# Stage 1 of two transforms in 64x64 products, with the cosine split and the order rewritten

## The chip, the core and the metric

One core of a Trainium2 chip runs the whole program. Its engines work from their own queues, each strictly in the order in which the program issued to it: TensorE (PE) multiplies matrices into PSUM, ScalarE (ACT) applies functions and copies results out of PSUM, VectorE (DVE) does elementwise work, GpSimd (POOL) does elementwise work between SBUF tensors, and SyncE (SP) issues the DMA transfers. The metric is the device time of one execution in microseconds; lower is better. The kernel before takes 498.01 us, the median of three runs (497.34 to 498.78).

## The reference

The model is a layer of two parts over 2048 tokens of 512 channels, in float32:

```python
x = A_u
h  = x + _A_ref(_layernorm(x), ...)     # a long convolution for each channel
h2 = h + _B_ref(_layernorm(h), ...)     # an expert layer

# _A_ref: K[d,l] = 2 Re sum_n C[d,n] exp(dt A)[d,n]^l   (128 modes for each channel)
#         y = irfft(rfft(u, 4096) * rfft(K, 4096))[:2048];  return y + u * D_skip
# _B_ref: for 32 heads: scores of two 16-entry key tables, the best of each,
#         expert index i1 * 16 + i2;  out = sum_h gelu(x . u[e_h]) v[e_h]
```

So a kernel K of 2048 taps has to be made for each of the 512 channels, both it and the normalized input are transformed to 4096 points, multiplied, and transformed back. Then comes the expert layer, with one expert of 256 for each of 32 heads and each token.

## The kernel before, in words

**First part, the convolution.** The 512 channels are worked in four groups of 128 (c = 0 to 3), and each group in four pieces of 32 channels (kt = 0 to 3). The taps of a channel come from two tables of powers that are multiplied with each other: 32 tables in all (i = 0 to 31, 16 channels each, two for one kt). For a table,

- POOL adds the phases `pg` (L557) from short tables of multiples, and multiplies the magnitudes `mg` (L588 and L594). For four tables together it first makes the short tables (`steps`, `bases`, `powers`, `heads`, L538 to L581).
- ACT takes sine (L647) and cosine (L644 and L645: absolute value, then a sine with a shift) of the phases into PSUM.
- DVE multiplies sines and cosines with the magnitudes, six instructions in four pieces (`sin_g`, `sin_f`, `cos_g`, `cos_f`, L651 to L664). The cosine pieces write over `mg`, the sine pieces write `gf`.
- PE multiplies the two factors (`kgen`, L690, the tile `kps`): 64 instructions for a table. ACT copies two tables' results to `k` (L698), DVE adds the skip term (L702).

`pg`, `mg` and `gf` have two buffers each, so table i can be written only when table i-2 has been used.

**The transforms** go in two stages of matrix products. Stage 1 (`stage1`, L463 to L477) multiplies 32 channels with the constant `c1_s`: the 128 partitions hold four channels of 32 positions, the constant is block diagonal in these four channels, and for each of eight groups g there are two products (real and imaginary part) of 128 rows, 64 output partitions and 128 columns. It runs for the input u (16 times, tile `s1u`, from `xs`) and for the taps (16 times, tile `s1k`, from `k`). Each run is two pieces on PE, of four groups each into one PSUM bank, each with a copy on ACT (L474) to `yu` or `yk`. Stage 2 (L488, tiles `s2yu` and `s2yk`) takes eight pieces for each c. The u result is copied to `U`; the k result is multiplied with U by DVE (`prod`, L732 to L735), for c = 3 with a part on ACT (L739) and on POOL (`rest`, L743). Then `ia` (L764) begins the inverse, and its results go to DRAM (`t_d`, L789) for c < 3 and stay in SBUF for c = 3.

Beside this the weights of the expert layer are folded with the keys (`w_piece`, L828 and L836, 32 pieces), from 512 KB loads on SP.

**Second part.** After the last ia the PSUM and SBUF pools are handed over and eight blocks of 256 tokens are worked: the end of the inverse (`ib`, L1036), layernorm, scores (L1150), selection by comparison (L1280), output. A few small constants are loaded for it (`small`, L938 to L940) and converted (`casts` and `plain`, L943 to L948), and the folded weights are read back from DRAM (`w_q`, L921) and split in a high and a low part (L924, L925).

**What sets the order.** Nothing is scheduled at run time. The function adds 1729 pieces to a plan, each with an engine, a planned cost in us and what it depends on; `plan.run(ORDER)` (L1348) then issues them in the written-out order `ORDER` (L34). The planned costs do not enter the run. Each engine's queue is the subsequence of ORDER that belongs to it. The PSUM pool `psA` has seven banks of 512 float32 for all of the first part.

Of the kernel before, what the change touches and what calls it, by code (L numbers as in the profile page):

```python
# [9 lines left out]
F32 = mybir.dt.float32  # L10
# [9 lines left out]
P = 128  # L20
# [7 lines left out]
def view(t, off, dims):  # L28
# [136 lines left out]
def kernel(ctx, tc, xa, xb, xt, lar, aim, cre, cim, ldt, dsk, wq, ka, kb, ue, ve,  # L165
# [294 lines left out]
    def flat(ps, m):  # L460
        return ps.rearrange("p a b -> p (a b)").rearrange("p (g m) -> p g m", m=m)

    def stage1(dst, lhs8, kt, nm, r, tiles, key):  # L463
        for n in range(2):
            job = {}

            def mm(n=n, job=job):
# [981 lines left out]
```

## Time and profile before

| | |
|---|---|
| median of three runs | 498.01 us (497.34 to 498.78) |
| profiled execution | 499.36 us, its span 497.4 us |
| PE busy | 444.8 us, 89% of the span, 7206 matmul instructions |
| DVE busy | 408.7 us, 82% |
| ACT busy | 296.6 us, 60% |
| POOL busy | 324.7 us, 65% |
| HBM | 46.08 MB read, 13.89 MB written |
| TensorE clock granted | 0.973 of full on average |

The span runs from the first to the last instruction of one execution on the chip. A group line gives busy time, the mean length of one instruction in ns, then the engine's idle time just before these instructions and what ended it. A wait line gives the total, the number and the longest. A stage line (a stretch in us) gives the busy time of each engine within it, the granted clock, the share of the DMA engines and GB/s; with a line number it counts that line alone. A line of time gives start, length and what ran. A float32 product counts as two matmul instructions, each with its own weight load.

### The profile page before, as it was taken

How to read it: one execution, taken by the hardware profiler on the slowest of the kernel's cores; microseconds unless marked ns; L12 is line 12 of the kernel's file. 1: busy time of each engine (PE TensorE's matmuls, PEld its weight loads, DVE VectorE, ACT ScalarE, POOL GpSimd, SP SyncE). 2: the span in 40 equal slices, each digit the busy share in tenths (PEclk: the TensorE clock that was granted, in tenths of full speed). 3: DMA queues.
4: the chain of work that ended last, by engine and by line, in shares of the span. 5: the costliest groups of instructions: out<-in, count | busy, mean ns of one | idle time of the engine just before them, and what ended most of it. 6: DMA issues, size and time to landing. Idle time of an engine off the chain costs nothing.

```text
span 497.4 us, 16692 instructions
## 1 busy us (share of the span) xinstructions
PE 444.8 (89%) x7206; PEld 389.8 (78%) x7206; DVE 408.7 (82%) x708; ACT 296.6 (60%) x594; POOL 324.7 (65%) x344
## 2 busy tenths in 40 slices
PE   0455789999999899999997799999999999999985
PEld 0233679999998889999996788887978888787874
DVE  4998998999879897899766764888979686978994
ACT  6865799859998669966985434463052331416231
POOL 3999899999999998988955203572263516536130
PEclk9977799999999999999999799999999999999999
DMA  7888924670153441400027458210170311010012
GB/s 291 336 270 290 370 64 142 210 253 29 43 193 99 133 130 47 171 3 3 1 88 254 153 179 285 84 47 1 67 246 29 125 49 43 1 45 0 1 54 77
DMA packets 27361, 61.04 MB, mean 123 GB/s; under 512 B 7028, under 2 KB 14456, under 8 KB 26136
## 3 DMA queue, kind: packets, MB, share of 16 engines
q1 hardware_dynamic: 27288, 59.98, 35.0%
q8 instruction: 56, 0.92, 0.8%
q14 instruction: 17, 0.14, 0.1%
HBM read 46.08 MB, written 13.89 MB: 121 GB/s over the span
## 4 chain that ended last, share of the span: by engine, by line
PE 66%; DVE 21%; ACT 4%; DMA 3%; POOL 3%; issue 2%; SPq 0%; DVEq 0%; ACTq 0%; POOLq 0%
PE sc L1150 14%; PE ia L764 12%; PE s2yu L488 6%; PE kps L690 5%; DVE oh L1280 5%; PE s1k L471 4%; PE xu L1157 4%; PE s1u L471 4%; PE s2yk L488 3%; PE ib L1036 3%; DMA wq<-wq 2%; PE o L1327 2%; PE cnt L1290 2%; PE wps L828 2%; DVE U L733 2%
## 5 line engine op out<-in xcount | busy, mean ns | idle before, releaser
L557 POOL TENSOR_TENSOR pg<-PS 128x1024 int32<-128x1024 int32 x32 | 68.8, 2151 | 0.1
L588 POOL TENSOR_TENSOR mg<-TS 128x1024 f32<-128x1024 f32 x32 | 62.5, 1959 | 9.3 <-PE kps L690 9.1
L1280 DVE TENSOR_SCALAR oh<-idxb,ec_s 128x2048 bf16<-128x2048 bf16 (+1 forms) x72 | 50.3, 757 | 6.8 <-ACT idxb L1262 6.8
L764 PE MATMUL ia<-ca_s,U 128*128 128x128 f32 x256 | 51.1, 282 | 0.5 <-POOL U L743 0.5
L1192 POOL TENSOR_TENSOR ks<-kq 128x512 f32<-128x512 bf16 x16 | 17.2, 1078 | 46.5 <-DVE kq L1186 45.5
L1060 POOL TENSOR_TENSOR vs<-hc 128x256 f32<-128x256 f32 x8 | 6.6, 829 | 61.8 <-ACT hc L1083 61.8
L645 ACT ACTIVATE t<-t,halfpi 128x512 f32<-128x512 f32 x64 | 42.4, 662 | 2.1
L1150 PE MATMUL sc<-w_hi,hhi 128*128 128x480 f32 x128 | 42.2, 410 | 0.0
L764 PEld LDWEIGHTS ia<-ca_s,U 128*128 128x128 f32 x256 | 40.3, 199 | 0.8 <-POOL U L743 0.8
L644 ACT ACTIVATE t<-pg 128x512 f32<-128x512 int32 x64 | 39.1, 610 | 2.5 <-DVE gf L652 2.2
L647 ACT ACTIVATE t<-pg 128x512 f32<-128x512 int32 x64 | 37.9, 609 | 2.9 <-POOL pg L557 1.3
L1150 PE MATMUL sc<-w_lo,hhi 128*128 128x480 f32 x128 | 38.4, 380 | 0.0
L1150 PE MATMUL sc<-w_hi,hlo 128*128 128x480 f32 x128 | 38.4, 381 | 0.0
L764 PE MATMUL ia<-ca_s,yk 128*128 128x128 f32 x192 | 38.2, 281 | 0.0
L594 POOL TENSOR_TENSOR mg<-TS 128x512 f32<-128x512 f32 x32 | 37.4, 1172 | 0.2
L828 PE MATMUL wps<-wq,ka_s 128*32 128x128 f32 x200 | 12.4, 326 | 25.1 <-DMA wq<-wq 22.0
L690 PE MATMUL kps<-mg 128*32 128x64 f32 x1024 | 33.5, 229 | 1.0 <-DVE mg L660 0.7
L488 PE MATMUL s2yk<-yk,c_s 128*128 128x128 f32 x256 | 32.6, 279 | 1.4 <-DVE U L735 0.7
L690 PE MATMUL kps<-gf 128*32 128x64 f32 x1024 | 32.9, 226 | 0.0
L471 PE MATMUL s1u<-c_s,xs 128*64 128x128 f32 x512 | 31.8, 276 | 1.1 <-DVE xs L508 0.7
L488 PEld LDWEIGHTS s2yk<-yk,c_s 128*128 128x128 f32 x256 | 30.2, 192 | 3.1 <-ACT yk L474 1.3
L488 PE MATMUL s2yu<-yu,c_s 128*128 128x128 f32 x256 | 31.4, 277 | 0.0
(198 smaller groups left out, 1390.9 us busy)
## 6 DMA issues: line engine op xcount, KB each, us to landing
wq<-wq SPq DMA_DIRECT2D x25, 512.0 KB, 4.8
t_d<-T SPq DMA_DIRECT2D x24, 256.0 KB, 3.9
Tb<-t_d SPq DMA_DIRECT2D x8, 768.0 KB, 7.1
x<-xa SPq DMA_DIRECT2D x8, 512.0 KB, 5.8
xs<-xb SPq DMA_DIRECT2D x16, 256.0 KB, 4.0
xt<-xt SPq DMA_DIRECT2D x8, 512.0 KB, 5.7
out<-ob SPq DMA_DIRECT2D x7, 512.0 KB, 3.0
c_s<-wq SPq DMA_DIRECT2D x4, 512.0 KB, 9.5
```

Of the source, the lines that this page charges most:

```text
L471: T.matmul(ps[64 * k:64 * k + 64, g, :], lhs8(4 * n + g), c1_s[:, k], start=True, stop=True)
L488: T.matmul(ps[:, k, :], c2_s[:, kk, :], y[:, :, kk, :], start=True, stop=True)
L557: G.tensor_tensor(view(pg, 0, [[32, 2 * NC], [8, 4], [1, 8]]), view(t["PS"], 1024 + off, [[1, 2 * NC], [128, 4], [0, 8]]), view(t["PS"], 8 ...
L588: G.tensor_tensor(view(mg, 0, [[96, NC], [8, 8], [1, 8]]), view(ts, 512 + 8 * o, [[8, NC], [1, 8], [0, 8]]), view(ts, 8 * o, [[8, NC], [0, ...
L594: G.tensor_tensor(view(mg, 64, [[96, NC], [8, 4], [1, 8]]), view(ts, 1536 + o, [[1, NC], [64, 4], [0, 8]]), view(ts, 1024 + 8 * o, [[8, NC ...
L644: A.activation(p, pg[:, :, k], AF.Abs)
L645: A.activation(p, p, AF.Sin, scale=-SINSCALE, bias=halfpi)
L647: A.activation(p, pg[:, :, k], AF.Sin, scale=SINSCALE)
L690: T.matmul(kps[32 * q:32 * q + 32, 2 * g + h, :], m[:, d, 64:96], m[:, d, 0:64], start=(e == 0), stop=(e == 1))
L764: T.matmul(ps[:, g, :], t[:, 4 * n + g].rearrange("p a b -> p (a b)"), ca_s[:, s, :], start=(s == 0), stop=(s == 1))
L1150: T.matmul(ps[:, 512 * h:512 * h + 480], t[x_][:, q, ts], I[w_][:, q, 480 * h:480 * h + 480], start=(q == 0 and x_ == w_), stop=(q == 3 an ...
L1280: V.tensor_scalar(oh[:, :, 0:ln], t["idxb"][:, :, sl], S["ec"][:, 4 * e + j:4 * e + j + 1], None, op0=ALU.is_equal)
```

## The change

Three things change.

*Stage 1.* The constant loses half its columns: instead of one block-diagonal block of four channels (128 columns) it holds two blocks of two channels, one in the upper 64 partitions and one in the lower 64 (64 columns). A group g now has four products, of 64 rows, 64 output partitions and 64 columns: row half h times real or imaginary part k. The row half h writes to bank h. All eight groups of a run are one piece on PE that takes two banks, with 64 matmul instructions in place of two pieces of 16. Each bank is then copied on its own by ACT; since a bank now holds two of the four channels d of every (g, k), the copy writes two elements out of every four.

*Cosine.* The absolute value and the shifted sine become two pieces of the plan, so that other ACT work can stand between them. The sines and cosines no longer follow each other through a common key.

*Order.* The plan has 1761 pieces and a new ORDER. On PE the ia pieces of c = 0 to 2 stand one to three at a time between the `kgen` pieces (before: in longer runs in places), and at the end of the first part stand kgen 30, kgen 31, stage 1 of pieces 1 and 3 of group 3, then stage 2; before: kgen 30, stage 1 of pieces 2, 1 (half) and 0, kgen 31, the rest of 1, and 3, then stage 2. On POOL `bases` of table 8 stands before `mg` of table 4 (before: after it). On DVE `casts` and `plain` stand ahead of the eight products of c = 3 (before: after the first copies of ia, c = 3). On SP the loads `small` come after the first t_d stores of c = 2 and one cb load, ahead of the w_q loads (before: after these). From ia of c = 3 on, the PE queue is the same but for a few places in the first blocks.

```diff
 ORDER = (
-    0, 17, 1, 2, 3, 4, 5, 6, 71, 72, 8, 16, 18, 19, 20, 21, 23, 24, 7, 87, 22, 29, 25, 35, 59, 36, 37, 30, 26, 38, 27,
...
+    0, 2, 1, 3, 4, 5, 71, 76, 66, 11, 9, 13, 87, 6, 18, 19, 17, 24, 20, 23, 27, 72, 25, 21, 22, 26, 29, 30, 35, 36,
...
-    c1_s = wk.tile([P, 2, 128], F32, name="c1_s")
+    c1_s = wk.tile([P, 2, 64], F32, name="c1_s")
...
     def stage1(dst, lhs8, kt, nm, r, tiles, key):
-        for n in range(2):
-            job = {}
-
-            def mm(n=n, job=job):
-                ps = bank(job, f"{nm}_{n}")
-                for g in range(4):
+
+        job = [dict(), dict()]
+
+        def mm():
+            ps = [flat(bank(job[h], f"{nm}_{h}"), 64) for h in range(2)]
+            for g in range(8):
+                for h in range(2):
+                    rows = slice(64 * h, 64 * h + 64)
                     for k in range(2):
-                        T.matmul(ps[64 * k:64 * k + 64, g, :], lhs8(4 * n + g), c1_s[:, k], start=True, stop=True)
-
-            def ev(n=n, job=job):
-                A.copy(dst()[:, 8 * kt + 4 * n:8 * kt + 4 * n + 4].rearrange("p g k d -> p g (k d)"), job["ps"])
-
-            k = plan.add("PE", 0.99, mm, r=r + ["c1"], t=tiles, take="psA", n_mm=16)
-            plan.add("ACT", 0.48, ev, w=[key + (kt, n)], t=tiles, give="psA", after=[k])
+                        T.matmul(ps[h][64 * k:64 * k + 64, g, :], lhs8(g)[rows], c1_s[rows, k], start=True, stop=True)
+
+        def ev(h):
+            A.copy(dst()[:, 8 * kt:8 * kt + 8].rearrange("p g k (h d) -> p h (g k) d", h=2)[:, h],
+                   job[h]["ps"].rearrange("p a b -> p (a b)").rearrange("p (a d) -> p a d", d=2))
+
+        k = plan.add("PE", 0.96, mm, r=r + ["c1"], t=tiles, take=("psA",) * 2, n_mm=64)
+        for h in range(2):
+            plan.add("ACT", 0.64, lambda h=h: ev(h), w=[key + (kt, h)], t=tiles, give="psA", after=[k])
...
-        def trig(k, cos):
-            p = t_k[k, cos] = flat(bank(t_k, f"t{k}{cos}_{i}", (k, cos, "ps")), 32)
-            pg = t["pg"]
-            if cos:
-                A.activation(p, pg[:, :, k], AF.Abs)
+        def trig(k, cos, part=0):
+            pg = t["pg"][:, :, k]
+            if part < 2:
+                t_k[k, cos] = flat(bank(t_k, f"t{k}{cos}_{i}", (k, cos, "ps")), 32)
+            p = t_k[k, cos]
+            if part == 1:
+                A.activation(p, pg, AF.Abs)
+            elif cos:
                 A.activation(p, p, AF.Sin, scale=-SINSCALE, bias=halfpi)
             else:
-                A.activation(p, pg[:, :, k], AF.Sin, scale=SINSCALE)
+                A.activation(p, pg, AF.Sin, scale=SINSCALE)
...
-            a = plan.add("ACT", cost, lambda k=k, cos=cos: trig(k, cos), r=[("pg", i)], w=["trig"], lag=0.2,
-                         t=tiles, take="psA")
+        for k, cos, fn, dcost in ((0, 0, sin_g, 1.2), (1, 0, sin_f, 0.6), (0, 1, cos_g, 1.2), (1, 1, cos_f, 0.6)):
+            a = plan.add("ACT", 0.61 if cos else 0.52, lambda k=k, cos=cos: trig(k, cos, cos), r=[("pg", i)], lag=0.2,
+                         t=tiles, take="psA", tab=None if cos else "trig")
+            if cos:
+                a = plan.add("ACT", 0.62, lambda k=k: trig(k, 1, 2), t=tiles, tab="trig", after=[a])
...
-    c1 = np.zeros((4, 32, 2, 32, 4))
+    c1 = np.zeros((4, 32, 2, 32, 2))
     for q in range(4):
-        c1[q, :, 0, :, q] = np.cos(a)
-        c1[q, :, 1, :, q] = -np.sin(a)
+        c1[q, :, 0, :, q % 2] = np.cos(a)
+        c1[q, :, 1, :, q % 2] = -np.sin(a)
```

More of the change, by code (lines that the diff above doesn't have):

```diff
@@ L664, in cos_f @@
             V.tensor_mul(mg[:, :, f_], mg[:, :, f_], t_k[1, 1])
-        for k, cos, cost, fn, dcost in ((0, 0, 0.52, sin_g, 1.2), (1, 0, 0.52, sin_f, 0.6),
-                                        (0, 1, 1.22, cos_g, 1.2), (1, 1, 1.22, cos_f, 0.6)):
-            a = plan.add("ACT", cost, lambda k=k, cos=cos: trig(k, cos), r=[("pg", i)], w=["trig"], lag=0.2,
-                         t=tiles, take="psA")
+        for k, cos, fn, dcost in ((0, 0, sin_g, 1.2), (1, 0, sin_f, 0.6), (0, 1, cos_g, 1.2), (1, 1, cos_f, 0.6)):
[3 more added lines that the diff above has]
+                a = plan.add("ACT", 0.62, lambda k=k: trig(k, 1, 2), t=tiles, tab="trig", after=[a])
             w = [("tab", i, k, cos)] + ([("mgf", i, k)] if cos else [])
@@ L1396, in _constants @@
     f = np.float32
-    return s, dict(c1=c1.reshape(128, 256).astype(f), c2=c2.reshape(128, 4096).astype(f),
+    return s, dict(c1=c1.reshape(128, 128).astype(f), c2=c2.reshape(128, 4096).astype(f),
                    ca=ca.reshape(128, 256).astype(f), cb=cb.reshape(128, 64, 64).astype(f),
```

164 rows, old and new, of the table ORDER are left out of this document.

## The prediction, made before the change was run

> **What bounds the kernel now.** I read the slices first, then busy time by stage, then who waits for whom, then the chain.
>
> ```profile
> PE   0455789999999899999997799999999999999985
> POOL 3999899999999998988955203572263516536130
> ```
>
> Forty slices of 12.4 us. GpSimd (POOL) is nearly full from the second slice to the twentieth, while it builds the 32 kernel tables; after that it is mostly idle and the second half belongs to TensorE (PE). Both lines are full in the same stretch, so the busy shares by stage are needed:
>
> ```profile
> core 0: us, PE busy (x) PEld busy (x) DVE busy (x) ACT busy (x) POOL busy (x), PEclk, DMA share, GB/s
> 60.00:255.00 195.00, 188.28 (x3685) 175.43 (x3687) 174.55 (x290) 164.67 (x319) 184.08 (x166) 1.00 0.30 102
> ```
>
> From 60 to 255 us PE works 188.3 of 195, POOL 184.1, VectorE (DVE) 174.6, ScalarE (ACT) 164.7. Two engines stand at the limit; the waits say which one holds the other.
>
> ```profile
> engine line waited for: us in total, times, longest us
> POOL mg L588 <- PE kps L690: 9.1, 6, 2.4
> ```
> ```profile
> 54.29 1.95 POOL L588 TENSOR_TENSOR mg<-TS 128x1024 f32<-128x1024 f32 x1 [2.20 <-PE kps L690]
> ...
> 191.44 1.96 POOL L588 TENSOR_TENSOR mg<-TS 128x1024 f32<-128x1024 f32 x1 [2.37 <-PE kps L690]
> ...
> 253.79 1.20 POOL L594 TENSOR_TENSOR mg<-TS 128x512 f32<-128x512 f32 x1
> 265.90 1.28 POOL L743 TENSOR_TENSOR U<-ki,U 64x512 f32<-64x512 f32 x1 [10.91 <-DVE yu L732]
> ```
>
> POOL's magnitude table `mg` has two buffers, so table i waits for the products `kps` of table i-2. PE reaches these late six times, 9.1 us in all: 2.2 at 54 us, the other 6.9 after 60. All else on POOL is its own work, back to back. So **POOL sets the pace until its last table piece ends at 255.0 (call that T), and PE, being late, takes 9.1 us of it.** The chain past T:
>
> ```profile
> 254.21 4.52 PE s1k L471 x80
> 258.72 1.03 PE kps L690 x64
> 259.75 2.90 PE s1k L471 x48
> ...
> 263.32 1.17 PE s2yk L488 x8
> ...
> 264.51 0.59 ACT ki L739
> ...
> 265.13 0.70 DVE yu L732
> ```
>
> From T to stage 2 (263.32) it is 8.3 us. Then DVE's eight products run back to back, and the rest (ia, and the whole expert part) hangs on their end.
>
> **The change, part by part.** *Stage 1 on PE.* A job (one transform, one channel group) was 32 instructions on 128 columns; it becomes 64 on 64 columns, each with half the rows. Now:
>
> ```profile
> 60.00:255.00 195.00, 53.00 (x880) 47.62 (x882) 1.00 0.30 102
> ```
>
> This is stage 1 (L471) alone: 53.00 us for 880 instructions, 60 ns each; back to back 4.52/80 = 56.5 ns, so 1.81 us a job. No row of before shows 64-row products side by side, so the new job is bounded. From below: L690 above issues 64 instructions on 64 columns, four column strips at once, in 1.03 us, 16.1 ns each. From above: if the two row halves take turns, only pairs overlap, and 32 pairs at the 64.4 ns that L690 takes for a group of four give 2.06 us. I take 1.03 us, because count, columns and four-fold packing are those of L690. In the stretch from 60 to 255 there are 880/32 = 27.5 jobs: 53.0 - 27.5 x 1.03 = 24.7 us less for PE, 163.6 instead of 188.3 us (upper bound: 27.5 x 0.25 = 7 us more). The Trainium skill has a rule against this: "TensorE: Matmul & The Clock Gate", Part 1, says that matmul starts never come closer than about 25 ns. By it the job would take 64 x 25 = 1.6 us, and PE would gain only about 6 us by that estimate. The row of L690, 16.1 ns, contradicts it for strips that work side by side.
>
> *What PE's 24.7 us are worth.* At most what POOL waited for PE, 9.1 us. They are spread over the whole stretch, 0.8 us at each job, against lateness of at most 2.4 us at a time, and the new order puts the inverse's ia pieces in ones, twos and threes between the kps instead of in runs. For the wait at 54 us the new order also sets one more piece of POOL work (`bases` of table 8, here at 71 us: 2.0 us together) ahead of that mg.
>
> ```profile
> 71.02 0.28 POOL L548 COPY PS<-A 128x128 int32<-128x128 int32 x1
> 71.38 1.71 POOL L550 TENSOR_TENSOR PS<-PS 128x128 int32<-128x128 int32 x3
> ```
>
> What remains: kps also waits for DVE's and ACT's table pieces, and DVE has 174.6 us to do in what becomes some 188, 93%.
>
> ```profile
> 80.00:180.00 100.00, 97.70 (x1935) 90.79 (x1935) 90.10 (x147) 81.52 (x162) 97.12 (x92) 1.00 0.38 126
> ```
>
> From 80 to 180 us POOL was 97.1% busy beside a PE at 97.7%, with hardly a wait. From 180 to 255:
>
> ```profile
> POOL mg L588 <- PE kps L690: 6.3, 4, 2.4
> ```
>
> I let the later part become like this one and leave 2.5 us of waits: **-6.6 us**. Ends: -9.1 and 0.
>
> *Evictions on ACT.* Each still moves 512 elements a partition, but writes runs of two elements in every four instead of one run of 512.
>
> ```profile
> 60.00:255.00 195.00, 31.34 (x56) 1.00 0.30 102
> ```
> ```profile
> L772 ACT COPY T<-ia 128x512 f32<-128x512 f32 x24 | 13.8, 592 | 1.2 <-PE ia L764 1.1
> L474 ACT COPY yk<-s1k 128x512 f32<-128x512 f32 x32 | 17.8, 592 | 1.6 <-PE s1k L471 1.4
> ```
>
> L474 in the stretch: 31.34/56 = 0.56 us each. L772 writes runs of four elements and takes the same 592 ns as L474's long run, so short runs alone cost nothing down to four. For two: from below 0.56, from above twice 592 = 1.18 us (a pair costs what four did). I take 0.72: the diff raises its planning price from 0.48 to 0.64, and the 0.16 is added to the row. ACT: 164.7 + 56 x 0.16 = 173.6 us, 92% of 188. It has cover: 0 on the end. The Trainium skill, "SBUF — State Buffer" (its note on SBUF cachelines), gives lines of 16 bytes that run at full rate with two hits each; two of four fp32 are two hits, so by it ACT would stay at 164.7. That changes no term of the sum, only the odds of a full ACT.
>
> *Cosine in two pieces.* The same two activations (L644, L645), now with room for other ACT work between them; no work is added. If the pieces are pulled apart, DVE gets a cosine later by one eviction, 0.6 us. The cover is DVE's other work:
>
> ```profile
> DVE gf L651 <- POOL mg L588: 4.1, 6, 1.5
> ...
> DVE mg L664 <- ACT t L645: 1.6, 4, 0.7
> DVE mg L659 <- ACT t L645: 1.6, 4, 0.5
> ```
>
> These are DVE's waits from 60 to 255 us (total, times, longest): it waited 3.2 us for cosines in 64 of them. 0; without the cover +1, two or three such delays at the last tables.
>
> *The tail past T.* L664 of the last table and kps stay as they are; after kps come k131 and k133 in 2 x 1.03 us instead of 2.90 (-0.8), but five evictions stand on ACT behind the last kps copy at about 0.64 apart instead of some 0.52 (+0.6): **-0.2 us**.
>
> ```profile
> 260.30 2.09 ACT L474 COPY yk<-s1k 128x512 f32<-128x512 f32 x4
> ```
>
>
> *A wait that the new order adds.* DVE's four small casts (`casts`, `plain`, L943 on) stood at 290 us, after ia began; now they stand ahead of the eight products. They need the three little loads of L938 to L940, which on SP's queue stand behind a run of t_d stores and one cb load.
>
> ```profile
> 290.27 0.18 DVE L943 CAST key_s<-key_f 128x30 bf16<-128x30 f32 x1
> ```
> ```profile
> 254.02 3.16 SPq L789 DMA_DIRECT2D t_d<-T  x4
> ...
> 264.03 2.56 SPq L789 DMA_DIRECT2D t_d<-T  x4
> ...
> 279.72 0.64 SPq L938 DMA_DIRECT2D key_f<-keys  x1
> 280.40 0.43 SPq L939 DMA_DIRECT2D ec_s<-ecode  x1
> 280.87 0.43 SPq L940 DMA_DIRECT2D hs_f<-hsel  x1
> ```
> ```profile
> hs_f<-hsel SPq DMA_DIRECT2D x1, 16.0 KB, 3.7
> ```
>
> The last eviction of ia2 stands on ACT just ahead of cosine of table 31, so the stores go out from about T+1.5; 2.6 to 3.2 us of issue, 0.4 for cb, and then 1.5 for the three: the last is issued near T+6.5 and, by 3.7 us, lands at T+10.2. The first product could start at 265.13 - 255.0 - 0.2 = T+9.9; the casts, about 0.5 us, end at T+10.7. Behind the casts wait all eight products, then POOL's L743, ia, everything. **+0.8 us**; ends 0 (the load lands early) and +4 (SP waits for freed memory).
>
> *Elsewhere.* c1 is half as large (one small DMA of many). The start is reordered, but POOL begins its tables near 8.7 us, after the same ka load; DVE's step of the first 64 modes comes first, so its new first piece should be fed in time: 0, ends -1 and +2.
>
> ```profile
> 8.39 0.21 POOL L280 TENSOR_TENSOR ka_s<-ka_s 128x15 f32<-128x15 f32 x1 [6.93 <-DMA ka_s<-ka]
> 8.57 0.21 POOL L280 TENSOR_TENSOR kb_s<-kb_s 128x15 f32<-128x15 f32 x1
> ```
>
> From ia3 on the queues are nearly unchanged: 0.
>
> Sum: -6.6 - 0.2 + 0.8 = -6.0. The profiled execution took 499.36 us (span 497.4 and 1.96 around it), 1.35 above the median of 498.01. 499.36 - 6.0 = 493.4, and at the median **492.0 us**.
>
> **Rivals.** (1) *All waits go*: POOL never waits, the casts are in time: 498.0 - 9.1 - 0.2 = 488.7. For it: PE falls to 87%. Against: DVE and ACT both go above 90%.
> (2) *The gain is hidden*: kps comes late through DVE or ACT instead, or the casts hold up 3 us or more, and POOL gets back 0 to 3 us: about 496. For it: DVE at 93% in a fixed order. Against: POOL's waits for kps are those that the trace names, and DVE itself waited 4.1 us for POOL's mg.
> (3) *ACT becomes the bound*, slower: without stage-1 evictions ACT has 164.7 - 31.3 = 133.3 us in the stretch; with 56 evictions of p us it fills the present 195 us at p = 1.10. From there the kernel is slower than before. At p = 1.18 ACT needs 199.4 us even if never idle: 498 + 4.4 = 502.4. Against: L772's 592 ns. The Trainium skill's "TensorEngine Tiling (Array Packing)", on the PSUM bottleneck, warns that the copy out of PSUM may take over once the products are packed; ACT's 85% in the stretch is the room there is.
> (4) *The row halves do not overlap*: jobs of 2.06 us, PE 188.3 + 7 = 195.3 us, so it is the bound with an order written for less: 498 + 7 = 505. Against: column strips do overlap in L690 (16.1 ns each).
>
> **How the numbers follow.** Forecast (489.5 to 494.5) 0.48; rival 1 0.14; rival 2 0.24; rival 3 0.06; rival 4 0.08. A measurement here tells 0.3% (1.5 us) from no change. Faster means below 496.5: 0.48 + 0.14 + 0.13 of rival 2 = 0.75; same is the remaining 0.11 of rival 2; slower is 0.14, rivals 3 and 4. Range 487.5 to 499.0: all of the forecast and of rival 2, nearly all of rival 1.
>
> **What would show it.** Right: stage 1 at about 1.0 us for 64 instructions; POOL's wait for kps below 4 us; T near 248.5; PE some 25 us less busy before T; ACT's L474 line between 0.6 and 0.8 us each. Wrong: a job near 1.8 or 2.0 us; L474's successor above 1.1 us; T unmoved; a DVE wait of several us for a small load (key_f or hs_f) ahead of the first product; or POOL waits of the old size with another name before them.

## The result, and the profile after

The changed kernel takes **513.51 us** (median of 4 runs, 511.23 to 514.53) beside 498.39 us for the kernel before on the same chip (497.34 to 499.05): ratio 1.0299, 95% interval 1.0259 to 1.0339. The forecast was 492.0, the range 487.5 to 499.0. The profiled execution has a span of 511.4 us, 14.0 more than before.

The slices of the changed kernel's page, 40 of 12.8 us, for TensorE and GpSimd:

```profile
PE   1556778989988979787996599999999999999986
POOL 3999888996999988996971601564053625445130
```

GpSimd has eights and sixes among its nines now and stays at its tables a little longer; TensorE, which stood at nine from the seventh slice to the twenty-first with one eight, now has sevens and eights there. Busy time by stage of the changed kernel (length; then busy us of PE, PEld, DVE, ACT and POOL with their instructions; granted clock, DMA share, GB/s), first the same 195 us as before, then up to the new end of the tables:

```profile
60.00:255.00 195.00, 168.18 (x4290) 153.41 (x4291) 165.67 (x270) 154.14 (x300) 174.86 (x157) 0.96 0.32 108
60.00:265.00 205.00, 178.18 (x4507) 162.98 (x4508) 174.15 (x284) 163.96 (x318) 184.73 (x163) 0.97 0.30 103
```

TensorE is busy 20 us less in the 195 us, and the other engines got less done too: GpSimd 174.9 us of work where it had done 184.1. It needs the next 10 us for the same 184.7. The last table piece, the start of stage 2 and the last ia, from the timeline (the first two rows) and the chain of the changed kernel:

```profile
263.72 1.15 POOL L600 TENSOR_TENSOR mg<-TS 128x512 f32<-128x512 f32 x1
...
275.72 8.83 PE L494 MATMUL s2yk<-yk,c_s 128*128 128x128 f32 x64 [1.20 <-ACT yk L478]
```
```profile
290.62 16.80 PE ia L774 x126
```

T is 264.87 where it was 254.99: **+9.9**. From T to stage 2 it is 10.85 us where it was 8.33: **+2.5**. From there to the last ia 14.90 for 13.99: +0.9. From ia to the end 220.8 for 220.1: +0.7. Together the 14.0 us. What GpSimd waited for from 60 us to T in the changed kernel (total, times, longest):

```profile
POOL mg L594 <- PE kps L700: 9.5, 7, 3.8
POOL pg L563 <- ACT t L656: 4.0, 1, 4.0
POOL mg L594 <- ACT t L656: 1.5, 1, 1.5
POOL mg L594 <- DVE xs L514: 0.9, 1, 0.9
POOL mg L594 <- DVE gf L661: 0.4, 1, 0.4
```

That is 16.3 us; in the same stretch of before it was 6.9 for kps and 0.2 for DVE. The waits for kps (the products of `kgen`; the expectations below call them the key products), which the change was to take away, have grown by 2.6. The larger part of the 9.2 us more is new: 5.5 for ScalarE, and 1.1 more for DVE. So TensorE, busy for less time, is later than before. Its own waits in the first 300 us of the changed kernel show what it is late for; "issue" means that it waited for nothing that the profile shows:

```profile
PE kps L700 <- issue: 5.8, 4, 2.2
...
PE s1u L475 <- issue: 4.4, 4, 2.1
PE s1k L475 <- issue: 2.1, 3, 1.2
```

12.3 us, in the two groups of products that have 64 columns. The kernel before has one such row in that stretch, 0.6 us in other products. These stretches of "issue" are called stops from here on. Eleven of them are over 0.25 us; nine lie on the chain of waits ahead of the last ia, 11.3 us together (before: one, 0.6). How one of these gaps sits on the path shows in the chain of waits of the changed kernel (start, length, what, how many products):

```profile
206.13 1.09 PE s1k L475 x64
207.22 0.57 PE wps L838 x16
207.80 1.81 PE s1k L475 x105
209.61 0.70 issue
210.31 0.57 PE s1k L475 x23
210.89 1.65 PE kps L700 x104
212.54 2.19 issue
214.73 0.59 PE kps L700 x24
```

After 185 products without a pause the engine stops inside a job, waiting for no other engine; it goes on for 127 products (23 + 104), stops again for 2.2 us, and goes on. The same happens behind T: the chain has 1.82 us of "issue" at 268.22 and 1.15 at 272.34 (rows below), 3.0 us together, which is more than the +2.5.

```profile
268.22 1.82 issue
270.04 0.97 PE kps L700 x51
271.01 1.33 PE s1k L475 x77
272.34 1.15 issue
```

51 + 77 = 128 products between the two. The DMA queue that brings instructions, of before and then of after (packets, MB):

```profile
q8 instruction: 56, 0.92, 0.8%
```
```profile
q8 instruction: 64, 1.05, 0.9%
```

The changed kernel's page counts 8230 products and as many weight loads on TensorE: 16,460 instructions in 64 packets, 257 each (before: 2 x 7206 in 56, 257). The 2048 instructions by which the two differ are 8 packets, 256 each. So a packet is about 128 products with their loads, if the queue serves mostly TensorE. That is the distance between the stops. The theory formed from this, called SUPPLY in the runs: *TensorE uses narrow products up faster than the packets come, and a long run of them empties its store.* Its rival, ORDER: *the written-out order is what costs the time, whatever the products are.*

### The profile page after: what moved, and what is told of

Its sections match the earlier page's. It is cut to its first block, busy times and chain, and to the rows that moved or that the text cites. A ratio compares the mean times of both kernels' runs of the same rounds, so it can differ in the third digit from the quotient of the medians.

```text
span 511.4 us, 18756 instructions
## 1 busy us (share of the span) xinstructions
PE 438.0 (86%) x8230; PEld 378.9 (74%) x8230; DVE 409.3 (80%) x708; ACT 296.3 (58%) x594; POOL 325.7 (64%) x344
## 4 chain that ended last, share of the span: by engine, by line
PE 51%; DVE 19%; ACT 10%; POOL 9%; issue 6%; DMA 4%; SPq 0%; DVEq 0%; POOLq 0%; ACTq 0%
PE sc L1160 11%; PE ia L774 9%; DVE oh L1290 4%; PE s2yu L494 4%; PE kps L700 4%; PE s2yk L494 3%; PE xu L1167 3%; PE s1u L475 3%; PE o L1337 2%; PE cnt L1300 2%; DVE U L743 2%; PE ib L1046 2%; ACT t L654 2%; PE s1k L475 2%; DMA wq<-wq 2%
## 5 line engine op out<-in xcount | busy, mean ns | idle before, releaser
L700 PE MATMUL kps<-mg 128*32 128x64 f32 x1024 | 36.2, 233 | 6.5 <-DVE mg L673 3.2
L700 PE MATMUL kps<-gf 128*32 128x64 f32 x1024 | 35.1, 230 | 4.0 <-issue 4.0
L494 PE MATMUL s2yk<-yk,c_s 128*128 128x128 f32 x256 | 35.3, 293 | 3.1 <-ACT yk L478 1.2
L494 PEld LDWEIGHTS s2yk<-yk,c_s 128*128 128x128 f32 x256 | 32.3, 204 | 4.6 <-ACT yk L478 1.3
L700 PEld LDWEIGHTS kps<-mg 128*32 128x32 f32 x1024 | 26.5, 116 | 11.8 <-issue 10.1
L494 PE MATMUL s2yu<-yu,c_s 128*128 128x128 f32 x256 | 33.4, 282 | 0.8 <-DVE U L745 0.8
L494 PEld LDWEIGHTS s2yu<-yu,c_s 128*128 128x128 f32 x256 | 30.8, 195 | 2.2 <-PE wpt L846 1.0
```

The lines of the kernel that those rows point to most:

```text
L494: T.matmul(ps[:, k, :], c2_s[:, kk, :], y[:, :, kk, :], start=True, stop=True)
L700: T.matmul(kps[32 * q:32 * q + 32, 2 * g + h, :], m[:, d, 64:96], m[:, d, 0:64], start=(e == 0), stop=(e == 1))
```

## The experiments

**Two orders, three kinds of product.** The change altered the products and the order at once. Four kernels take them apart. The first keeps the order of before; each run's two pieces become one, at the place of the first:

```
 ORDER = (as before, stage-1 pairs merged at the first one's place)
 stage1: as in the changed kernel (64x64 products, two banks, strided copies); cosine in one piece
```

> Stage 1 in 64x64 products with its strided copies, but the order of before (each stage-1 run stands where its first half stood) and the cosine in one piece. Two theories. SUPPLY: PE runs out of instructions after long runs of narrow products (idle time on PE that nothing in the trace ends), and PE's lateness then reaches ACT, DVE and POOL. It expects such gaps here too, 5 to 12 us in sum, and 496 to 506 us. ORDER: the new order is what costs, the products are fine. It expects no gaps that matter, POOL waiting under 4 us for kps, and 489 to 494 us.

The second has the changed kernel's order with the products of before:

```
-  T.matmul(ps[h][64*k:64*k+64, g, :], lhs8(g)[rows], c1_s[rows, k], ...)   # 32 products of 64 columns
+  T.matmul(ps[n][64*k:64*k+64, g, :], lhs8(4*n + g), c1_s[:, k], ...)      # 16 products of 128 columns
```

> The kernel after (new order, cosine split), but each stage-1 run does the products of before: 16 products of 128 rows and 128 columns (32 instructions) into two banks, and two copies in long runs. SUPPLY expects no gap over 0.5 us without a releaser on PE; PE has some 25 us more to do, so 500 to 509 us, below the 513.5 of after. ORDER expects no gain from it: 513 us or more, since PE is slower and the order the same.

The third and fourth leave stage 1 out as a computation:

```
+  T.matmul(ps[h][64*k:64*k+64, g, :], bf16(lhs8(..)), bf16(c1_s[:, k]), ...)  # 16 products of 256 columns
```

> The kernel after, but stage 1 is left out as a computation: each run fills the same two banks with 16 bf16 products of 256 columns (16 instructions in place of 64, about 0.9 us of PE time in place of 1.03; the values are not the transform's). Copies, order and cosine as after. SUPPLY expects 488 to 497 us and hardly a gap without a releaser. ORDER expects 510 to 515 us, as after.

> As oldorder_64, but stage 1 is left out as a computation: 16 bf16 products of 256 columns in each run, the same banks and strided copies. It shows what 25 us less of PE work are worth in the order of before without the narrow instructions. SUPPLY expects 488 to 493 us and several us less than oldorder_64; ORDER expects the same time as oldorder_64 within 1.5 us.

| | before's products (32 instructions a run) | 64x64 (64 instructions) | bf16 (16 instructions) |
|---|---|---|---|
| order of before, two pieces | 498.4 | not run | 499.0 (below) |
| order of before, merged | 514.9 (below) | 517.01, ratio 1.0348 [1.0308, 1.0389] | 509.87, 1.0204 [1.0153, 1.0256] |
| new order | 519.63, 1.0375 [1.0311, 1.0438] | 513.51, 1.0299 [1.0259, 1.0339] | 499.57, 1.0014 [0.9992, 1.0036] |

None of the four times is in the range that SUPPLY gave for it, and of those that ORDER gave only that of the second run is (513 us or more). So neither theory is right as it stood. In the new order the same place, banks, copies and cosines cost nothing against before when stage 1 has few instructions, and 13.9 us more when it has many. The two have nearly the same work on TensorE from 60 to 255 us: stage 1 alone in the bf16 kernel and in the changed kernel (length; PE and PEld busy with instructions; clock, DMA):

```profile
60.00:255.00 195.00, 33.72 (x464) 25.37 (x464) 0.98 0.31 107
```
```profile
60.00:255.00 195.00, 36.29 (x1728) 31.73 (x1728) 0.96 0.32 108
```

33.7 and 36.3 us busy, 464 and 1728 instructions. 2.6 us of work do not by themselves make 13.9 us of time. What differs much is the number of instructions, and the form of the products, which the next run keeps. The granted clock differs too: from 80 to 120 us it is 0.91 in the changed kernel and 1.00 in the bf16 one; what that is worth was not taken apart. In the bf16 kernel GpSimd waits 2.9 us for kps from 60 us to T, and T is 252.9:

```profile
POOL mg L600 <- PE kps L706: 2.9, 2, 2.2
```

But that kernel does not reach 492 either. Its last ia starts at 274.25 us, 3.1 earlier than before; the rest takes 222.9 us for 220.1, and in it TensorE stops for 2.6 us at ib (before: 0.4). ORDER is wrong for the loss in the new order, and SUPPLY alone does not explain the missing gain. With the products of before the new order is slowest of all, as ORDER had it: GpSimd waits 13.8 us for kps and 8.5 for ScalarE there. That this order was written for runs of 1 us and gets runs of 1.8 is a likely reason that no run shows. That kernel also has a stop of 2.3 us at s1u, where SUPPLY gave none over 0.5; it comes 21 products behind 128 kps products in a row. The new order sets two kps jobs side by side in three places; the order of before does so once. In the merged old order every column is slow, 11.5 us even with bf16; that is taken up below.

**Half the instructions, the same tiles.** Bf16 also changes the form of the products. The next run keeps fp32, the 64x64 tiles, banks, copies and order, and gives each product 128 columns, so that 32 instructions move the same columns. Every second group is computed with its neighbour's weights.

```
-  for g in range(8):  T.matmul(ps[h][.., g, :], lhs8(g)[rows], c1_s[rows, k], ...)                  # 64 columns
+  for g in range(4):  T.matmul(ps[h][.., g, :], lhs8(2*g)[rows], c1_s[rows, k] twice side by side)  # 128
```

> The changed kernel with its 64x64 tiles, its banks, its strided copies and its order, but every stage-1 run made of 16 fp32 products of 128 columns in place of 32 of 64 columns: half the instructions (32 for 64), and by the estimate 32 instructions of 128 columns over four tiles the same columns through the array. What is left out: every second group of eight is computed with the weights of its neighbour. Theory SUPPLY (TensorE runs out of instructions in long runs of narrow products): the idle time of TensorE without a releaser behind stage-1 and key-product lines falls from 12.3 us in the first 300 us to under 5, GpSimd's waits for the key products from 11.4 us to about 4 to 6, and the time from 513.5 to 498 to 505 us. Rival TILES (products in 64x64 tiles themselves hold up the products around them, however many instructions they are): idle time and waits stay, 510 to 515 us. Rival ORDER (the new order alone costs the time): 510 us or more.

506.74 us (505.58 to 508.66), ratio 1.0157 [1.0110, 1.0204]: 6.8 us below the changed kernel with equal work, and 7.2 above the bf16 one; just over the upper end that SUPPLY gave, as are GpSimd's waits for kps (7.5 us, where 4 to 6 were expected). TensorE's gaps in the first 300 us of this kernel:

```profile
PE s1u L475 <- issue: 3.8, 1, 3.8
...
PE kps L701 <- issue: 0.9, 1, 0.9
...
PE s1k L475 <- issue: 0.7, 1, 0.7
```

5.4 for 12.3 us, in three stops, each soon after one of the three runs of 128 kps products in a row (they begin at 101.6, 208.7 and 263.1 us). The rival that 64x64 tiles are themselves in the way falls; 64, 32 and 16 instructions a run give 513.5, 506.7 and 499.6. The last ia starts at 290.62, 283.88 and 274.25 us in these three, and the stops on the chain ahead of it are 11.3, 5.4 and 1.6 us. So of the 16.4 us between the first and the third 9.7 are stops that stand on the chain; the rest is not placed by these runs. A part may be what follows from a stop: GpSimd's long wait for ScalarE, which ends at 123 to 129 us, is 4.0 us in the changed kernel, 5.7 here and 7.4 with the products of before, each time behind stops at 104 to 112 us, and the bf16 kernel has neither; how one leads to the other was not followed.

**The products by themselves.** A program of its own runs narrow products back to back on data that lies ready, with 12 wide products ahead of each section.

> A program of its own, not the kernel: after 12 wide products each, five runs of TensorE alone on data already in place: (a) 384 fp32 products in four column strips of 32, 128 rows, 64 columns, the form of the key products; (b) 384 in 64x64 tiles of 64 columns, the form of the changed stage 1; (c) 192 of 128 rows, two column tiles of 64, 128 columns, the form of the stage 1 before; (d) 192 in 64x64 tiles of 128 columns; (e) the strips of (a) again while 12 loads of 512 KB run. It computes nothing of the reference. Theory SUPPLY expects (a) and (b) to start at about 16 ns per instruction for the first hundreds of instructions and then to break up into stretches with idle gaps of 0.5 to 2.5 us, about 3.4 us for each 256 instructions in the long run (768 instructions: over 12.4 us by one gap or more), no gap in (c), at most a short one in (d), and (e) not better than (a). If (a) and (b) run through in about 12 to 13 us without a gap, SUPPLY in this form is wrong and the gaps have to do with the kernel around them.

The timeline of the second section, 64x64 tiles with 64 columns, then sections three and four (128 columns; 128-row products, then 64x64 tiles):

```profile
58.02 2.79 PE L53 MATMUL b<-a 64*64 64x64 f32 x175
61.71 2.09 PE L53 MATMUL b<-a 64*64 64x64 f32 x128 [0.90 <-issue]
65.44 2.09 PE L53 MATMUL b<-a 64*64 64x64 f32 x128 [1.64 <-issue]
69.17 2.09 PE L53 MATMUL b<-a 64*64 64x64 f32 x128 [1.64 <-issue]
72.62 2.09 PE L53 MATMUL b<-a 64*64 64x64 f32 x128 [1.36 <-issue]
```
```profile
99.28 21.18 PE L58 MATMUL b<-a 128*64 128x128 f32 x384
...
140.82 10.71 PE L63 MATMUL b<-a 64*64 64x128 f32 x384
```

175 products run through, then exactly 128 at a time, with a stop between. Inside a stretch a product takes some 16 ns; from the start of one stretch to the next it is 3.45 to 3.73 us, or 27 to 29 ns a product. Sections three and four have no stop: 21.18/384 = 55 ns, and 10.71/384 = 27.9 ns, which is just what the supply gives. Stops in total, of the sections with 32-wide strips, with 64x64 tiles, and with strips beside 6 MB of loads:

```profile
PE b L73 <- issue: 10.1, 5, 3.1
PE b L45 <- issue: 7.7, 5, 1.7
PE b L53 <- issue: 6.9, 5, 1.6
```

This is SUPPLY without the kernel around it; beside the loads the stops are 2.4 us longer, in this one execution.

The trace also has the packets of the instruction queue, 16,384 bytes each. In the second section:

| packet, from and to (us) | TensorE goes on at | after the packet's end |
|---|---|---|
| 59.36 to 60.40 | 61.71 | 1.31 |
| 62.84 to 64.14 | 65.44 | 1.30 |
| 66.56 to 67.89 | 69.17 | 1.28 |
| 70.30 to 71.25 | 72.62 | 1.37 |

Each stop ends 1.3 to 1.4 us after a packet has come in, and the next packet starts 1.1 us after TensorE goes on. It is so in the kernels as well: the two stops behind T in the changed kernel end 1.44 and 1.41 us after packets that came in at 268.60 and 272.08 us, and in all 18 profiles 97 of the 98 stops of over 0.25 us end 1.2 to 1.6 us after a packet. So what TensorE waits for in a stop is instructions. The Trainium skill, "Runtime: NRT & Kernel Launch", section "Instruction fetch mechanics", says that instructions are refilled in blocks of 16 KiB (256 instructions), and that this is hidden because engines dispatch more slowly than the refill. The trace agrees with the block (stops 128 products apart, 16.4 KB a packet) and not with the hiding: 256 instructions are used up in 2.09 us and refilled in 3.45 to 3.73.

**What the relief of TensorE is worth.** The kernel before, with nothing changed but the bf16 products: two pieces, one bank each, contiguous copies, same order, TensorE's stage 1 busy for 36.0 us in place of 53.0 in the 195.

```
-  T.matmul(ps[64*k:64*k+64, g, :], lhs8(4*n + g), c1_s[:, k], ...)            # 8 fp32 products a piece
+  T.matmul(ps[64*k:64*k+64, g, :], bf16(lhs8(..)), bf16(c1_s[:, k]), ...)     # 8 bf16 products, 256 columns
```

> The kernel before with nothing changed but the products of stage 1: two pieces, one bank each, the contiguous copies and the order all stay; each piece is 8 bf16 products of 256 columns in place of 8 fp32 products of 128 columns, so that stage 1 as a computation is left out and TensorE is relieved by some 0.4 us per piece, 64 pieces. This is the relief that the prediction counted on, without narrow products and without a new order. The prediction's own term (waits of GpSimd for the key products go, -6.6 us) expects 490 to 493 us and waits of GpSimd for key products under 3 us. Theory ORDER in its strong form (a written-out order gives back what one engine gains) expects 496 us or more, the waits still near 9 us. An addition of time is expected by neither.

498.99 us (496.81 to 503.06, 10 runs), ratio 1.0002 [0.9972, 1.0031]: **nothing**. GpSimd's waits in the first 300 us of this kernel:

```profile
POOL mg L595 <- PE kps L697: 3.6, 3, 1.7
POOL mg L595 <- DVE k L709: 3.1, 1, 3.1
```

The waits for kps fell by 5.5 us. But at 55 us a wait of 3.1 us for DVE stands where one of 2.2 us for kps stood, so all these waits together fell from 9.3 to 6.7 us, by 2.6 where the prediction counted 6.6. Stage 2 starts at 260.36, 3.0 earlier. These 3 us are gone at the end. Its chain of waits, in the second part:

```profile
354.57 1.67 PE ib L1043 x119
356.24 2.27 issue
358.52 0.35 PE ib L1043 x9
```

The inverse's last step, ib, has 128 narrow products in a run; here they stop after 119 of them.

**Where the packets end.** In the kernel before there is 0.4 us of such stops at ib. Is that chance? The same kernel profiled again:

> The kernel before, unchanged, profiled once more: whether the idle gaps of TensorE in the inverse transform's narrow products of the second part (0.4 us in the first profile of this kernel, 1.6 to 6.5 us in four of the other runs) come and go between executions of one program. If they do, this profile shows 1 us or more there, or its second part (from the last quarter's inverse transform to the end, 220.1 us in the first profile) differs by over 1 us; if they belong to the edited kernels, it shows 0.4 us and 220 us again.

499.04 us, span 497.1, 0.4 us of stops at ib again. So they look like a property of the program, as far as two profiles can tell. If they depend on where a packet ends, moving all instructions on by part of a packet must move them. One early product group, in an idle stretch, is done three or five times over:

```
-  for a, k_s in ((0, ka_s), (1, kb_s)):
+  for a, k_s in ((0, ka_s), (1, kb_s)) * (3 if n == 0 else 1):      # or 5
```

> As oldorder_halves_few (the kernel before, stage 1 as a computation left out: two pieces, their banks, copies and order as before, bf16 products of 256 columns), and the first product group of the key weights, at 9.7 us, is done three times in place of once, with the same result: 64 more instructions with their weight loads, while TensorE waits for a load there (idle from 10.8 to 16.3 us). All later instructions of TensorE stand 64 further on in their stream, a quarter of a 256-instruction packet. Theory BLOCK (the idle gaps inside the narrow products of the second part, 2.3 us in oldorder_halves_few, depend on where a packet of 256 instructions ends within them) expects the gaps in those narrow products of the inverse transform to change by 1 us or more, and the time with them: 496 to 498 us if they go, 500 to 502 us if they grow. Rival STATE (they depend on how fast TensorE got there, not on the place in the stream) expects 2 us of gaps again and 498 to 500 us.

> As few_shift2 with five times in place of three: 128 more instructions, half a packet. BLOCK expects gaps that differ from those of oldorder_halves_few and of few_shift2 by 1 us or more in at least one of the two, and a time that follows; the prediction's term for the relief of TensorE alone (3.0 us that the first part did gain) would then show as 495.5 to 497 us in the one without gaps. STATE expects 2 us and 498 to 500 us.

> The kernel before with the first product group of the key weights done five times in place of once: the same result, 128 more instructions of TensorE in an idle stretch. BLOCK expects idle gaps of 1.5 us or more in the second part's narrow products, where the kernel before had 0.4 in both of its profiles, and 499.5 to 502 us; if the shift costs the first part nothing and the gaps stay away, 498 to 499 us, as STATE expects.

> The changed kernel with the same shift of 128 instructions. SUPPLY (sustained supply is below what long runs of narrow products ask for) expects the gaps in the first part to move but not to go: 10 to 14 us of idle time without a releaser in the first 300 us, and 511 to 516 us. If the place in the packets were all there is to it, the time falls to 505 us or below, or rises over 519.

With 64 instructions more, the bf16 kernel takes 496.14 us (494.19 to 502.91, 8 runs), ratio 0.9951 [0.9924, 0.9978]: faster than before by 2.4 us, though its interval just touches that of the unshifted kernel. The profile has one stop at ib, 0.9 us just ahead of 300 us, where there were 2.5 us, and stage 2 starts 0.5 us later than without the shift:

```profile
260.85 7.41 PE L495 MATMUL s2yk<-yk,c_s 128*128 128x128 f32 x64 [0.88 <-ACT yk L481]
```

From the last ia to the end this kernel takes 494.5 - 274.83 = 219.7 us; without the shift it was 499.2 - 274.35 = 224.9. The 1.6 us less of stops are a part of these 5.2 and not all: the profiled execution without the shift was itself 2.0 us above the median of its kernel. With 128 more it takes 497.99 (ratio 0.9980 [0.9958, 1.0003]); no stop at ib is left here, but its last ia starts 3.4 us later, after new waits at 47 to 72 us that I cannot explain. The kernel before with 128 more takes 499.57, 1.0015 [0.9995, 1.0034]: no stop appeared at ib, against what BLOCK gave, but 1.7 us of them at kps. The changed kernel with 128 more takes 518.10 (513.44 to 521.71, 6 runs), 1.0374 [1.0331, 1.0416]: some 4 us slower than without, above the 511 to 516 that SUPPLY gave. Its profiled execution took 521.71, the longest of the six, so only the times are used. So the place in the stream moves stops about, and in two of the four shifts the time moved too, by some 2.4 us down and some 4 up. But it does not decide alone: in the shifted kernel before a packet comes in from 297.92 to 299.34 us, among the ib products, and no stop goes with it.

**What merging the pieces costs.** The new form of stage 1 takes two banks in one piece. The kernel before with its own products, merged:

```
-  k = plan.add("PE", 0.99, mm, ..., take="psA", n_mm=16)            # twice, four groups each
+  k = plan.add("PE", 0.96, mm, ..., take=("psA",) * 2, n_mm=64)     # once, eight groups
```

> The kernel before with its own 128x128-column products and contiguous copies, but the two pieces of each stage-1 run as one piece that takes two banks at once, at the place of the first. Nothing is left out. With products of few columns left out the same merged order took 509.9 us, with the 64x64 products 517.0. Theory MERGE (taking two banks in one piece at the place of the first half is what costs the old order its time: waits for the second half's data or for a free bank come ahead of the key products) expects 508 to 516 us, and GpSimd's waits for the key products of 10 to 25 us. Rival FEW (the merged order is harmless at the durations it was written for) expects 497 to 501 us. If it is slower than oldorder_64, narrow products cost the merged order nothing net.

514.90 us (513.38 to 515.71), 1.0304 [1.0262, 1.0346], GpSimd's wait for kps 16.5 us in the first 300, both in the ranges that MERGE gave. No work was added, and the time grew by 15.9 us. Not all of it arises at the merged pieces: the last ia starts at 287.95 us, 10.6 later than before, and from there to the end it is 224.45 us for 220.1, with these stops at ib, where before has 0.4:

```profile
PE ib L1036 <- issue: 6.5, 3, 2.8
```

So merging costs 10.6 us in the first part, and 4.4 go with stops in products that were not touched. TensorE's waits of this kernel from 60 to 255 us begin with

```profile
PE s2yk L488 <- DVE mg L660: 3.7, 2, 2.0
```

The products of stage 2 read nothing of `mg`; DVE's step on `mg` gives back the bank of a cosine. In the kernel before this row does not exist. Is it the place or the two banks? One piece at the place of the second half:

> As oldorder_128_merged (the kernel before, its own products and contiguous copies, the two pieces of a stage-1 run made one that takes two banks), but the one piece stands at the place of the second half, not of the first; its first eviction follows it, and eight evictions that it would have come behind are moved to the next place that they can stand at. Nothing is left out. Theory PLACE (at the first half's place the second half's 1 us of products, 64 times, comes ahead of work that GpSimd waits for) expects GpSimd's waits for the key products back at 8 to 12 us from 16.5, and 498 to 505 us. Rival BANKS (two banks taken at a time hold up the pieces behind, wherever the one stands) expects the waits to stay at 14 us or more, and 508 to 516 us.

511.97 us (510.69 to 512.87), 1.0278 [1.0256, 1.0301], wait for kps 15.1. The last ia starts at 287.60, and from there to the end it is 220.5 us, with these stops at ib:

```profile
PE ib L1036 <- issue: 1.7, 1, 1.7
```

So the 3 us between the two kernels lie behind the last ia, beside 4.8 us less of stops; ahead of it the place gives back 0.3 of the 10.6 us. That speaks for BANKS, in the range that it gave; it does not show it, since the piece is also 1.8 us long in one go, and no run has one without the other.

**The other two parts of the change.** Contiguous copies in the changed kernel (numbers land in the wrong place):

```
-  A.copy(dst()[:, 8*kt:8*kt+8].rearrange("p g k (h d) -> p h (g k) d", h=2)[:, h], ...)
+  A.copy(dst()[:, 8*kt+4*h:8*kt+4*h+4].rearrange("p g k d -> p g (k d)"), job[h]["ps"])
```

> The changed kernel with its copies from the bank to the spectrum contiguous (512 numbers in a row) in place of strided by pairs. What is left out: the numbers land at the wrong place, so that the spectrum is a permuted one. The prediction's term (the strided copies take 0.05 to 0.16 us more and are hidden behind GpSimd) expects the copies at 0.57 to 0.60 us in place of 0.64 and 510 to 515 us, within 2 us of the changed kernel. Rival ACT (ScalarE, for which GpSimd waits 5.5 us in the changed kernel, is made late by the strided copies): 505 to 510 us.

512.74 us, 1.0312 [1.0274, 1.0349]: no difference from the changed kernel. The copies of the two, changed kernel first (busy, mean ns of one):

```profile
L478 ACT COPY yu<-s1u 128x512 f32<-128x512 f32 x32 | 19.0, 649 | 12.5 <-PE s1u L475 12.3
```
```profile
L478 ACT COPY yu<-s1u 128x512 f32<-128x512 f32 x32 | 17.6, 595 | 14.6 <-PE s1u L475 14.6
```

Pairs in every four cost 54 ns a copy, and ScalarE is waiting for TensorE anyway. The cosine in one piece again:

```
-  part 1: Abs          part 2: Sin
+  part 1: Abs, Sin     part 2: nothing
```

> The changed kernel with the cosine's two activations back to back again: the absolute value and the sine both at the place where the new order puts the sine... no, at the place where it puts the absolute value, with nothing at the place of the sine. Nothing is left out. The prediction's term (the split is worth nothing) expects 510 to 517 us, no difference from the changed kernel beyond 2 us. Rival: the split is what lets ScalarE's evictions in between, and without it the evictions and GpSimd's waits for ScalarE (5.5 us in the changed kernel) grow: 516 to 522 us. Rival: the split itself holds VectorE up, and without it the time falls to 505 to 510 us.

517.85 us (514.75 to 518.20), 1.0384 [1.0351, 1.0418], about 4 us slower than the changed kernel. By the times the split gains in this order, in the range of the rival that expected this. The two profiled executions differ by 1.2 us only (spans 512.6 and 511.4), so where the 4 us arise is not seen.

## Why the prediction was wrong

**What bounds the kernel** was read right: GpSimd's last table piece sets the pace, and its waits for kps are what TensorE can change. The changed kernel shows its loss in GpSimd's waits too, 9.2 us more of them from 60 us to T; but only 2.6 of these are for kps, and 5.5 are for ScalarE, on which the prediction put nothing.

**The step that failed is "Stage 1 on PE".** The job was priced at 1.03 us from kps' row of 64 products. That price is nearly right for one undisturbed job: 64 weight loads in 1.02 us and 64 products in 1.09, row halves side by side, and the doubt about 16 ns was rightly dropped for a short run. But kps stood among wide products in the kernel before; the change puts narrow stage-1 runs next to narrow kps, and nothing in the sum priced a *run* of narrow products: the longest run of 64-column products before 290 us is 384 in the changed kernel (at 207.7 and 264.4 us) and 128 in the kernel before. The average over the stretch is harmless (195 us for 4290 products are 45 ns each, and supply gives one in 27 to 29); it is the bursts that stop, after 175 to 231 narrow products in the probe. Cost: 13.9 us between 16 and 64 instructions a run in the same order, with 11.3 us of stops on the chain for 1.6. Instead of 24.7 us less, stage 1 has 53.0 - 36.3 = 16.7 us less busy time in the 195 us: 1728 instructions are 27 jobs, 1.34 us each for the 1.03 priced, at a mean clock of 0.96, and stops on top. The 24.7 also set busy time, 53.0/27.5 = 1.93 us a job, against a back-to-back price; back to back on both sides it is 27.5 x (1.81 - 1.03) = 21.5.

**What PE's 24.7 us are worth** (-6.6) failed too, by itself: the relief without narrow stage-1 products gives 0, or at best -2.4 us at another place in the stream. The waits for kps fell as forecast in one profile (9.1 to 3.6 us, and to 6.1 and 4.7 in the two shifted ones); but with those for DVE that stand there now, GpSimd's waits for both in the first 300 us are 6.7, 7.2 and 8.8 us at the three shifts, where they were 9.3 and 2.5 was forecast. The step left out these other waits, and that the second part, costed at 0, is sensitive to where the instruction stream stands.

**Moving the pieces** had no term. Merging them in the old order costs 10.6 us ahead of the last ia, 15.9 in all. The new order takes that up for short runs, as far as these runs show: with bf16 products it is back at 499.6, with the products of before it is not (519.6).

**Evictions** 0.72 us each: 0.60 by the same count (32.44 us for 54; 31.34 for 56 before), near the lower bound, and hidden, as forecast (contiguous copies change nothing). **Cosine** 0: worth about -4 us in the new order, by the times. **Tail** -0.2: +2.5, for the 3.0 us of stops. **The added wait** +0.8 did not come. The casts waited 2.2 us for the small load, but ended before the first product could start, because `ki` on ScalarE was later still:

```profile
274.04 0.18 DVE L953 CAST key_s<-key_f 128x30 bf16<-128x30 f32 x1 [2.21 <-DMA key_f<-keys]
274.63 0.18 DVE L954 CAST hs_s<-hs_f 128x32 bf16<-128x32 f32 x1 [0.40 <-DMA hs_f<-hsel]
...
278.44 0.69 DVE L742 TENSOR_TENSOR yu<-s2yk,U 128x512 f32<-128x512 f32 x1 [3.36 <-ACT ki L749]
```

**Second part** 0: +0.7, right for this kernel; in other runs it moved by up to 4.8 us, so part of that is luck. **Rivals**: two of them, 3 and 4, were on the slower side, and neither is what happened: ScalarE is at 79% in the stretch (154.1 of 195), and the row halves overlap (1.09 us for the 2.06 of rival 4). Rival 2, the hidden gain, is what the relief alone did. No rival had TensorE itself starving.

## What to carry to other kernels

Splitting a product into more and smaller ones is priced by two numbers: the time of one job, and the rate at which instructions arrive; compare the second with the longest run of narrow products that the order makes, neighbours included, not with the average. Before counting on an engine's relief in a hand-written order, leave its work out once (here bf16 products in its place) and time that: it bounds what any faster form can give. And a piece that takes two banks where two pieces took one each is a change of its own.

## What the runs showed that I had not expected

- TensorE can run dry of instructions: 175 products in a row go through in the 64x64 section of the probe (199 and 231 in the two strip sections), then 128 at a time, 3.45 to 3.73 us apart, while the same products take 2.0 to 2.1 us. A stop ends 1.2 to 1.6 us after a packet of 16,384 bytes has come in. 128-column products in 64x64 tiles, at 27.9 ns, just keep pace.
- The stops at ib were the same in both profiles of before (0.4 us) and move when the stream is shifted by 64 or 128 instructions: the same kernel gave 498.99, 496.14 and 497.99 us at three shifts. What besides the place in the stream decides whether a stop comes is open.
- One piece that takes two banks in place of two that take one each, with no work added, cost 13 to 16 us in an order written for single banks: 10.3 and 10.6 us ahead of the last ia at either place, the rest behind it.
